# Attention with column norms and a soft mixture of experts on one core: loads of turned v replaced by turns on TensorE, and a new order of all steps

## The chip, the cores and the metric

One core of a Trainium2 chip runs the whole program. The metric is the device time of one execution in microseconds (us). The program is built once; all four engines that compute, and the DMA queue that SP feeds, get their instructions in an order fixed by the source, and only semaphores hold them back.

## The reference, cut to what matters

```python
# q, k, v: (4, 5056, 256); norms and softmax over columns
qn = q / (norm(q, axis=1) + 1e-6);  kn = k / (norm(k, axis=1) + 1e-6)
a  = softmax(kn.T @ qn / tau)                    # (4, 256, 256)
x  = (v @ a).reshape(20224, 256)
logits = x @ phi                                 # 32 slots
d  = softmax over all 20224 rows;  slot_in = d.T @ x
slot_out[e] = relu(slot_in[e] @ w1[e]) @ w2[e]   # 8 experts, 4 slots each
out = softmax over the 32 slots (logits) @ slot_out
```

x is never formed: `logits = v @ (a @ phi)`, and `d.T @ x = (d.T @ v) @ a`.

## The kernel before, in words

Each of the four batches is cut into 10 units of 512 rows of q and k together (1 MB each, tile `raw`, five buffers) and into 5 pieces of 1024 rows of v (1 MB each, tile `v`, six buffers, the last three pieces in buffers of `raw`). For a unit u, ACT squares it (`square`, L203) and rounds its first half to fp32r (`cast`, L182), DVE takes the rest of that half (`low`, L188) and adds the squares up (`add`, L209), and TensorE adds the scores of the four row groups j into the bank `S` (`score`, L226): j = 0, 1 from `hl`, j = 2, 3 from `raw` directly. When a batch's ten units are done, the steps `att_...` turn squares and scores into the 256x256 softmax and into `M`, which is `a @ phi`.

The logits of a piece p (`logits`, L378) need v turned, channels on partitions, in two halves m = 0 and m = 1 (tiles `vt0`, `vt1`, three buffers each; `x` for the last pieces). A half comes in one of two ways. If (p, m) is in the set `LT` (L26), `load_vt` (L130) loads it from a copy of v that the host has turned, 512 KB (480 KB for the last piece of a batch). If not, `turn` (L348) and `turned` (L354) are planned twice, once for each 512 rows: four transposes of 128x128 on TensorE into a bank, and one copy of 128x512 by ACT out of it. After the logits come their running maximum, exponentials, `weights` (L462) and `gather` (L477, the sum of v by slot), and after the last piece `last_slots` and `last_back` (L573): the slots' input.

Then the experts: `up` (L636, needs the tiles of w1), `relu`, `flip_h`, `back_h` (L661; x = 0 on DVE, x = 1 on ACT), `down` (L668; half h needs the loads of w2 of that half), `o_copy`, `o_fold`, `o_back`. Beside them DVE and ACT work on the softmax over slots of each batch b (`c_max`, `c_sub`, `c_exp`, `c_sum`, `c_rec`, `c_mul`, `c_flip`, L578 to L611). Last come the outputs, one tile of 1 MB per piece: `out_mul` (L702) on TensorE, four `out_evict` (L722) shared by ACT and DVE, and `store` (L738). The five pieces of batch 0 are stored in halves, the first half as soon as `o_back(0)` is done.

What sets the order: every step is put into a list `plan` with a key that is not used any more, and the list `ORDER` (L31) is a written-out sequence of positions in `plan`; the last loop calls the steps in that sequence. So the order of each engine's queue is that of `ORDER`, and so is the order in which SP issues the loads and stores. A load takes the buffer of its tag that came free first among the steps already listed, and waits for the last reader of what lay in it.

Of the kernel before, what the change touches and what calls it, by code (L numbers as in the profile page):

```python
# [22 lines left out]
NU = B * UB  # L23
NRAW = 5
NS = [0] + [2] * (NU - 1)
LT = {(p, 0) for p in range(15)} | {(p, 1) for p in range(0, 15, 3)} | {(p, 0) for p in range(15, 20)} | {(10, 1), (13, 1), (15, 1)}  # L26
GR = {b: (3, 2) for b in range(B)}

ORDER = [  # L31
# [46 lines left out]
]  # L78


# [1 line left out]
def colnorm_attention_soft_moe(  # L82
# [671 lines left out]
    def at(key, f, *a):  # L754
        plan.append((key, len(plan), f, a))
# [27 lines left out]
    for p in range(15):  # L783
        for h in range(2):
            for m in range(2):
                if (p, m) in LT:
                    continue
# [67 lines left out]
    for p in range(17):  # L855
        k = (4, 6, 8, 10, 12, 15)[p] if p < 6 else 2 * p + 7
        for h in range(2):
# [3 lines left out]
            if h:  # L861
                for m in range(2):
                    if (p, m) in LT:
                        at(k + h + 0.996 + 0.001 * m, load_vt, p, m)
# [9 lines left out]
    for p in (17, 18, 19):  # L874
        at(NU + 0.99, load_v, p)
        for m in range(2):
            if (p, m) in LT:
                at(NU + 0.99, load_vt, p, m)
    for p in (15, 16, 17, 18, 19):
        for h in range(2):  # L880
            for m in range(2):
                if (p, m) in LT:
                    continue
# [176 lines left out]
```

## Time and profile before

| | us |
|---|---|
| three runs | 288.46, 290.16, 293.66 |
| median | 290.16 |
| span of the profiled execution | 288.4 |

The page gives the profiled execution's span alone as its time, from its first to its last instruction. "Busy" is the time in which an engine had at least one instruction under way; PE is TensorE's matmuls, PEld its loads of weights. A line of the profile is a source line of the kernel. "DMA" is the mean busy share of the core's 16 DMA engines (it can read a little above 1).

### The profile page before, as it was taken

The page shows a single profiled execution, that of the slowest core. Times are in us where ns is not written, and L with a number is a line of the kernel's source. Part 1 is how long each engine was busy: PE and PEld are TensorE (multiplying, and loading weights), DVE is VectorE, ACT ScalarE, POOL GpSimd, SP SyncE. Part 2 cuts the span into 40 slices and gives each one's busy share as a digit, 9 for nine tenths or more (in the row PEclk, how much of TensorE's full clock was granted, in tenths as well). Part 3 has the DMA queues.
Part 4 walks back from the last instruction along what each step waited for, and adds up shares of the span by engine and source line. Part 5 has one row for each costly group of instructions (what it writes and reads, how often), then busy time and mean ns, then how long its engine had stood idle before and what let it go on. Part 6 is the DMA issues. An engine that isn't in the chain of part 4 may idle for free. (4 is left out here: it accounts for less than half of the span.)

```text
span 288.4 us, 6095 instructions
## 1 busy us (share of the span) xinstructions
PE 251.8 (87%) x2452; PEld 203.7 (71%) x2452; DVE 236.4 (82%) x389; ACT 185.1 (64%) x264; POOL 9.8 (3%) x10
## 2 busy tenths in 40 slices
PE   6899999999999999999999999999889898884000
PEld 6689998898888879778788686786554777763000
DVE  1299999899999999999999999988768678994100
ACT  2799887889799796687867957175613426863200
POOL 0000000400004000000200000100000000000000
PEclk9799999999999999999999999999999999998555
DMA  6999999999999999999999999999999997999995
GB/s 206 416 411 421 389 403 427 424 414 418 381 419 367 389 424 424 421 421 422 419 406 419 405 416 427 425 427 417 420 415 413 414 369 311 402 428 413 424 422 245
DMA packets 20188, 115.61 MB, mean 401 GB/s; under 512 B 2368, under 2 KB 2368, under 8 KB 9664
## 3 DMA queue, kind: packets, MB, share of 16 engines
q1 hardware_dynamic: 20160, 115.22, 97.7%
q8 instruction: 19, 0.31, 0.4%
q14 instruction: 9, 0.07, 0.1%
HBM read 94.24 MB, written 20.97 MB: 400 GB/s over the span
## 5 line engine op out<-in xcount | busy, mean ns | idle before, releaser
L203 ACT ACTIVATE sq<-raw 128x2048 f32<-128x2048 f32 x40 | 76.3, 1911 | 18.1 <-DVE sq L209 6.4
L209 DVE TENSOR_TENSOR sq<-sq,sq 128x1024 f32<-128x1024 f32 (+1 forms) x63 | 85.2, 1365 | 1.3 <-ACT sq L203 0.6
L226 PE MATMUL S<-raw 128*128 128x256 f32 x328 | 81.7, 389 | 2.7 <-DMA raw<-in_qk_dram 2.7
L226 PE MATMUL S<-hl 128*128 128x256 f32 x468 | 71.2, 298 | 0.1
L226 PEld LDWEIGHTS S<-raw 128*128 128x128 f32 x328 | 60.1, 194 | 13.4 <-DMA raw<-in_qk_dram 3.5
L226 PEld LDWEIGHTS S<-hl 128*128 128x128 f32 x468 | 61.1, 190 | 3.4 <-issue 1.2
L188 DVE TENSOR_TENSOR hl<-raw,hl 128x1024 fp32r<-128x1024 f32 x39 | 46.8, 1213 | 9.7 <-ACT hl L182 9.7
L182 ACT CAST hl<-raw 128x1024 fp32r<-128x1024 f32 x39 | 40.2, 1042 | 2.6 <-PE S L226 1.7
L736 DVE COPY o<-op_None 128x512 f32<-128x512 f32 x30 | 18.7, 674 | 7.9 <-issue 7.2
L734 ACT COPY o<-op_None 128x512 f32<-128x512 f32 x30 | 15.8, 593 | 12.5 <-issue 8.2
L712 PE MATMUL op_None<-so,cT 32*128 32x256 f32 x240 | 18.6, 401 | 1.9 <-ACT o L734 1.4
L485 PE MATMUL G<-v,dn 128*32 128x256 f32 x320 | 20.1, 382 | 0.1
L712 PEld LDWEIGHTS op_None<-so,cT 32*128 32x128 f32 x240 | 14.6, 184 | 5.6 <-ACT o L734 2.7
L378 PE MATMUL L<-vt,M 128*32 128x256 f32 (+1 forms) x272 | 17.7, 380 | 1.0 <-ACT M L332 1.0
L356 ACT COPY vt<-vTp 128x512 f32<-128x512 f32 x18 | 10.4, 583 | 11.1 <-PE vTp L351 11.1
L248 POOL TENSOR_TENSOR rn<-rn,half 128x4 f32<-128x4 f32 x4 | 9.1, 2263 | 176.2 <-DVE rn L243 176.2
L485 PEld LDWEIGHTS G<-v,dn 128*32 128x32 f32 x320 | 10.0, 109 | 6.5 <-issue 0.5
L351 PE MATMUL vTp<-ident,v 128*128 128x128 f32 x96 | 14.1, 276 | 0.0
L378 PEld LDWEIGHTS L<-vt,M 128*32 128x32 f32 x272 | 8.1, 109 | 7.1 <-ACT M L332 1.5
L351 PEld LDWEIGHTS vTp<-ident,v 128*128 128x128 f32 x96 | 11.0, 142 | 2.4 <-issue 1.2
L399 ACT COPY lt<-L 128x256 f32<-128x256 f32 x20 | 7.2, 372 | 7.6 <-DVE mxs L405 3.4
L734 ACT COPY o<-op 128x256 f32<-128x256 f32 x20 | 6.3, 380 | 8.0 <-PE op L712 8.0
(111 smaller groups left out, 252.8 us busy)
## 6 DMA issues: line engine op xcount, KB each, us to landing
raw<-in_qk_dram SPq DMA_DIRECT2D x39, 1024.0 KB, 9.2
v<-in_v_dram SPq DMA_DIRECT2D x20, 1024.0 KB, 10.6
out_dram<-o SPq DMA_DIRECT2D x15, 1024.0 KB, 12.3
vt<-in_vt_dram SPq DMA_DIRECT2D x21, 512.0 KB, 8.9
w<-in_moe_w_dram SPq DMA_DIRECT2D x8, 1024.0 KB, 14.4
w<-in_moe_w_dram SPq DMA_DIRECT2D x16, 512.0 KB, 11.1
out_dram<-o SPq DMA_DIRECT2D x10, 512.0 KB, 4.2
vt<-in_vt_dram SPq DMA_DIRECT2D x4, 480.0 KB, 10.1
```

The costliest lines, as they stand in the source:

```text
L182: act.copy(hl[:, :ns, 0::2, :], raws[u][:, :ns])
L188: dve.tensor_tensor(hl[:, :ns, 1::2, :], raws[u][:, :ns], hl[:, :ns, 0::2, :].bitcast(F32), op=ALU.subtract)
L203: act.activation(sq, raws[u], AF.Square)
L209: dve.tensor_tensor(a[:, lo:hi], a[:, lo:hi], s[:, lo:hi], op=ALU.add)
L226: pe.matmul(sm, w, x, start=first, stop=False, skip_group_check=True)
L351: pe.transpose(tp[:, P * jj : P * jj + P], vs[p][:, 4 * h + jj, P * m : P * m + P], ident)
L356: act.copy(x[:, h * UT : h * UT + UT], tps[p, h, m])
L378: pe.matmul(L[S * g : S * g + S, :n, :], M[:, m, :], x[:, :n, S * g : S * g + S], start=m == 0, stop=m == 1,)
L485: pe.matmul(gp[S * g : S * g + S, :C], dn[:, x, j, :], vt[:, j, :], start=x == 0 and j < G, stop=x == n - 1 and j >= G,)
L712: pe.matmul(ops[b, p, hf, g][:, h, :], cT[b][S * g : S * g + S, 4 * i : 4 * i + 4, :].rearrange("s j t -> s (j t)"), so[S * g : S * g + S] ...
L734: act.copy(dst, src)
L736: dve.tensor_copy(dst, src)
```

## The change

`LT` gets a term, and `ORDER` is another sequence:

```diff
-LT = {(p, 0) for p in range(15)} | {(p, 1) for p in range(0, 15, 3)} | {(p, 0) for p in range(15, 20)} | {(10, 1), (13, 1), (15, 1)}
+LT = {(p, 0) for p in range(15)} | {(p, 1) for p in range(0, 15, 3)} | {(p, 0) for p in range(15, 20)} | {(10, 1), (13, 1), (15, 1)} - {(3, 1), (6, 1), (9, 1), (10, 1), (13, 1), (15, 1)}
 ORDER = [
-    1, 0, 2, 5, 3, 4, 13, 7, 8, 9, 10, 23, 6, 14, 16, 15, 31, 606, 18, 22, 17, 19, 25, 24, 21, 27, 36, 32, 41, 12,
...
-    991, 1013, 1012, 1009, 1019, 1015, 1020, 1018, 1021,
+    0, 3, 5, 1, 4, 2, 13, 14, 7, 8, 12, 11, 22, 23, 9, 10, 31, 32, 16, 17, 20, 40, 41, 18, 21, 19, 25, 26, 30, 29, 27,
...
+    962, 1025, 1029, 1027, 1026, 983, 985, 987, 986, 1028, 984, 1007, 1009, 1008, 1011, 1010, 964, 1012, 953, 955,
+    957, 954, 988, 956, 958, 1030, 994, 940,
 ]
```

The old list has 1022 positions and the new one 1031. Read back through `plan`, the two give these sequences at the places that the prediction speaks of (qk5 is the load of unit 5, v4 that of piece 4, vt0,1 that of the half (0, 1)):

```
SP's queue, first loads after units 0 to 4
before  qk5 qk6 vt0,1 qk7 vt3,1 qk8 qk9 few qk10 qk11 qk12 v0 qk13 v1 qk14 qk15 qk16 v2 qk17 vt0,0 qk18 vt1,0 vt2,0 qk19 qk20 v3 ...
after   qk5 qk6 qk8 qk7 qk12 few qk9 v4 qk10 v1 qk11 qk15 qk13 qk14 v2 vt0,1 qk16 qk17 qk20 v0 vt0,0 vt1,0 qk18 qk19 vt2,0 vt3,0 qk23 qk21 ...

turns that only the new list has, with the PE steps beside them
 score31,0 turn11,0,1 att_turn2,0 att_turn2,1 turn10,1,1 score33,0 score32,0 turn10,0,1 att_phi2
 score39,3 shift2,0 turn13,1,1 score39,1 score39,0 finish_fold1 score38,2 score35,1 turn13,0,1 finish_slots1
 att_turn3,0 att_turn3,1 turn15,0,1 turn18,1,1 att_phi3 turn15,1,1 logits17

PE from last_slots on
before  up0,0 up0,1 up1,0 flip_h0,1 flip_h0,0 up1,1 down0,0 x3 flip_h1,0 flip_h1,1 down0,0 down1,0 x4 o_fold0
        out_mul0,0 down0,1 out_mul0,1 out_mul0,2 down0,1 out_mul0,3 down0,1 x2 down1,1 x4 out_mul0,4 o_fold1
after   up1,0 up0,1 up0,0 up1,1 flip_h0,1 flip_h0,0 flip_h1,1 flip_h1,0 down0,0 x4 down1,0 x4 o_fold0
        out_mul0,0 out_mul0,1 out_mul0,2 out_mul0,3 down0,1 x4 down1,1 x4 out_mul0,4 o_fold1

DVE from last_back to o_copy0
before  c_flip0,2 c_flip1,0 c_max3 c_sum2 c_sub3 c_flip1,3 c_rec2 back_h0,0 c_flip1,4 c_mul2 back_h1,0 c_flip1,1 c_flip1,2 c_sum3 o_copy0
after   c_flip0,1 c_sub2 c_max3 c_rec1 c_mul1 c_flip1,2 c_flip1,1 c_flip1,3 c_sum2 c_flip1,4 c_flip1,0 back_h0,0 c_sub3 back_h1,0 c_rec2 o_copy0

stores (batch, piece, half)
before  0,0,0 0,1,0 0,2,0 0,3,0 0,4,0 0,0,1 0,1,1 0,3,1 0,2,1 1,0 1,2 1,4 2,1 1,1 1,3 2,3 2,0 0,4,1 2,2 3,1 3,0 2,4 3,2 3,3 3,4
after   0,2,0 0,0,0 0,1,0 0,3,0 0,4,0 0,2,1 0,1,1 2,4 0,3,1 1,4 0,0,1 2,1 3,3 1,0 2,0 3,0 3,2 1,1 1,3 3,1 2,2 1,2 3,4 2,3 0,4,1
```

No function and no buffer count is changed.

## Rows read from the trace of the kernel before

**Rows 1.** The page's parts on busy time and on slices: busy time of each engine with its share of the span and its instructions; the busy share of the DMA engines in 40 slices of 7.2 us.

```profile
PE 251.8 (87%) x2452; PEld 203.7 (71%) x2452; DVE 236.4 (82%) x389; ACT 185.1 (64%) x264; POOL 9.8 (3%) x10
DMA  6999999999999999999999999999999997999995
```

**Rows 2.** Busy time by stage: the stretch, its length, busy us and instructions of PE, PEld, DVE, ACT and POOL, the granted TensorE clock, the DMA share, GB/s.

```profile
20.00:196.00 176.00, 174.89 (x1441) 147.30 (x1440) 171.77 (x248) 136.64 (x169) 9.05 (x4) 1.00 1.01 413
196.00:215.00 19.00, 16.54 (x211) 10.46 (x214) 14.07 (x50) 8.48 (x27) 0.00 (x0) 1.00 1.01 416
...
235.00:245.00 10.00, 9.04 (x198) 7.59 (x194) 7.26 (x21) 4.69 (x15) 0.00 (x0) 1.00 0.82 326
...
255.00:265.00 10.00, 7.45 (x94) 5.88 (x94) 8.01 (x15) 5.15 (x10) 0.00 (x0) 0.97 1.02 424
```

**Rows 3.** All waits of PE and of DVE from 20 to 196 us: who waited for whom, us in total, times, the longest.

```profile
PE L L378 <- ACT M L332: 0.6, 2, 0.4
PE nn L238 <- DVE sq L232: 0.2, 1, 0.2
...
DVE dn L466 <- ACT lt L456: 1.1, 1, 1.1
DVE rn L252 <- POOL rn L248: 0.9, 1, 0.9
```

**Rows 4.** Waits of SP's queue over the whole span, the two largest of the loads of `raw` (L120), in the same columns.

```profile
SPq L120 <- PE S L226: 56.9, 23, 8.7
...
SPq L120 <- DVE hl L188: 31.3, 17, 5.3
```

**Rows 5.** DMA issues by target and size: how many, KB each, median us from issue to landing; and the bytes read and written in all.

```profile
raw<-in_qk_dram SPq DMA_DIRECT2D x39, 1024.0 KB, 9.2
...
vt<-in_vt_dram SPq DMA_DIRECT2D x21, 512.0 KB, 8.9
w<-in_moe_w_dram SPq DMA_DIRECT2D x16, 512.0 KB, 11.1
...
raw<-in_qk_dram SPq DMA_DIRECT2D x2, 256.0 KB, 2.8
```

```profile
HBM read 94.24 MB, written 20.97 MB: 400 GB/s over the span
```

**Rows 6.** PE's instructions in order of time around one turn: start, us from the first start to the last end, instructions merged into one row. A row may start before the one above has ended.

```profile
95.93 0.60 PE L351 MATMUL vTp<-ident,v 128*128 128x128 f32 x4
96.36 1.03 PE L226 MATMUL S<-raw 128*128 128x256 f32 x4
97.04 1.06 PE L226 MATMUL S<-hl 128*128 128x256 f32 x6
```

**Rows 7.** The turns over the whole span, by line: instructions, busy us and mean ns of one, idle time of the engine just before them.

```profile
L351 PE MATMUL vTp<-ident,v 128*128 128x128 f32 x96 | 14.1, 276 | 0.0
...
L356 ACT COPY vt<-vTp 128x512 f32<-128x512 f32 x18 | 10.4, 583 | 11.1 <-PE vTp L351 11.1
```

**Rows 8.** DVE's work on the softmax over slots, and its evictions of the half stores of batch 0, by line, in the same columns.

```profile
L608 DVE STREAM_TRANSPOSE cT<-nat 128x256 f32<-128x256 f32 x20 | 8.6, 431 | 0.0
...
L736 DVE COPY o<-op 128x256 f32<-128x256 f32 x20 | 7.3, 414 | 2.8 <-PE op L712 2.7
...
L598 DVE TENSOR_TENSOR nat<-nat,cs 128x1280 f32<-128x1280 f32 x4 | 5.9, 1474 | 0.0
L583 DVE TENSOR_TENSOR nat<-nat,cm 128x1280 f32<-128x1280 f32 x4 | 5.9, 1473 | 0.0
L590 DVE TENSOR_REDUCE cs<-nat 128x40 f32<-128x1280 f32 x4 | 5.9, 1466 | 0.0
L580 DVE TENSOR_REDUCE cm<-nat 128x40 f32<-128x1280 f32 x4 | 5.9, 1463 | 0.0
...
L595 DVE RECIPROCAL cs<-cs 128x40 f32<-128x40 f32 x4 | 1.6, 403 | 0.1
```

**Rows 9.** All engines in order of time from the last pieces to the second half of the experts' output (a bracket: idle time before, and what ended it).

```profile
196.95 1.07 PE L378 MATMUL L<-vt,M 128*32 128x256 f32 x16 [0.43 <-ACT M L332]
...
214.51 0.19 DVE L574 COPY slT<-slp 128x32 f32<-128x32 f32 x1
...
214.87 5.36 PE L642 MATMUL H<-w,slT 128*32 128x512 f32 x48
...
221.25 1.92 PE L642 MATMUL H<-w,slT 128*32 128x512 f32 x16
...
221.35 0.69 DVE L664 COPY hT<-hTp 128x512 f32<-128x512 f32 x1 [0.81 <-DMA w<-in_moe_w_dram]
...
225.50 2.39 PE L673 MATMUL O<-w,hT 128*32 128x128 f32 x80
...
227.96 0.29 DVE L686 COPY ob<-O 128x128 f32<-128x128 f32 x1
...
229.15 0.73 PE L712 MATMUL op<-so,cT 32*128 32x128 f32 x16 [0.35 <-ACT so L694]
...
235.26 1.67 PEld L673 LDWEIGHTS O<-w,hT 128*32 128x32 f32 x60 [0.37 <-DMA w<-in_moe_w_dram]
```

**Rows 10.** SP's queue in order of time: the last loads and the first stores.

```profile
201.87 23.64 SPq L631 DMA_DIRECT2D w<-in_moe_w_dram  x15
230.76 12.80 SPq L744 DMA_DIRECT2D out_dram<-o  x9
```

86 rows, old and new, of the table ORDER are left out of this document.

## Prediction

> **What bounds the kernel now.** I read the page's slices first. The DMA engines are at nine tenths or more in nearly every slice [rows 1], and by stage their share is 1.01 at 413 to 424 GB/s wherever loads or stores stand ready [rows 2]. So bytes set a floor. Next the engines: from 20 to 196 us PE has a matmul under way for 174.89 of 176.00 us and DVE is busy for 171.77 [rows 2], and the list of waits gives PE 0.8 us in all and DVE 2.0 [rows 3]. So in this stage DMA, PE and DVE are all full at once; ACT, at 136.64, is not.
>
> Which of them has cover? A 1 MB load of `raw` lands 9.2 us after its issue [rows 5], while 1.05 MB at 0.42 MB/us takes 2.5: 6.7 us are the queue ahead of it. SP waits for buffers nearly always (56.9 us for PE's last score of a unit, 31.3 for DVE) [rows 4]. The loads run as far ahead as five buffers let them, and PE hardly ever waits for one.
>
> At the end the order matters. The last part of w2 ends PE's last wait at 235.26 [rows 9]; from there 20.97 MB of stores at 424 GB/s take 49.5 us [rows 2, 5], and 235 to 245 us runs at a share of 0.82, so 1.8 us are lost there. 235.2 + 49.5 + 1.8 = 286.5, and 1.9 remain to the span of 288.4: the end. The median of the three runs is 290.16, 1.8 above the span, and I add that to each sum.
>
> **The change, part by part.** First, how many loads go. Python's `-` binds before `|`, so the subtracted set acts on the last term alone and empties it: (3,1), (6,1), (9,1) come back in through the second term. **Three** loads are dropped. The lengths of the list agree: a half that is turned has four steps in place of one, and 1031 − 1022 = 9 is three halves.
>
> *DMA:* three times 512 KB, 1.57 MB; at 0.42 MB/us −3.7 us. The w2 loads would land at 231.5 if nothing else held the stream.
>
> *PE:* six turns more, 24 transposes. One turn starts at 95.93 and the next instruction at 96.36: 0.43 us [rows 6], so 6 × 0.43 = 2.6. The two of piece 15 lie beside `att_phi3`, before logits that waited 0.43 us for ACT's M [rows 3, 9], and are costed at nothing; if M is ready by then they cost 0.9. The four others fall where PE never waits: **+1.7 us** by the time of `last_back`. The row of transposes has a mean of 276 ns each [rows 7], but four in a row take 0.43 to the next issue, as they overlap. The Trainium skill, "TensorE: Matmul & The Clock Gate", section "Part 4: PE-mode transpose", gives about 275 ns for one 128x128 transpose in a kernel; by that, added up, 24 would take 6.6 us and not 2.6. As a duration the trace agrees with it (276), and the starts here decide.
>
> *ACT:* six copies of 583 ns [rows 7], 3.5 us, hidden in the 39 us for which ACT stands idle in that stage [rows 2]. A bank's next turn may wait for one; the copy's wait for PE is ACT's idle time (11.1 us) and not PE's.
>
> *DVE:* no work added. c_sub2, c_rec1 and c_mul1 (1.47 + 0.40 + 1.47 = 3.3 us [rows 8]) move from before `last_back` to behind it, so ahead of it DVE has 3.3 us less, PE sets the pace alone, and DVE will wait for it.
>
> *Loads in a new order:* SP's queue stands behind every buffer that is not free. Units 12, 15, 20 and 23 are asked for earlier than they are used, each holding one of five buffers. 176 us hold some 38 units, 4.6 us each; one buffer held for one unit makes later loads 4.6 us late, and the cover is 6.7. So one hold costs nothing, two together up to 2.5 us. I take nothing; the upper end is a rival below. POOL's four operations, which DVE awaited for 0.9 us [rows 3], keep their place.
>
> *The experts:* `last_back` was at 214.51 [rows 9], now 216.2. From there to `back_h`(0,0) DVE had three flips, three big operations and a reciprocal: 3 × 0.43 + 3 × 1.47 + 0.40 = 6.1 us, which is the 221.35 of before with its wait of 0.81. It now has six flips, four big ones and a reciprocal, 8.9 us [rows 8]: 225.1. The ups (5.36 + 1.92 us of PE [rows 9]) and two flips are done by 224.7, so DVE decides, if narrowly; ACT's c_exp2, now ahead of all `relu`, waits only for the second of those DVE steps. Then back_h0,0 (0.69), c_sub3 and back_h1,0 end at 228.0, and `down` of the second half of the hidden units runs behind them (64 matmuls at 2.39/80 us, 1.9 us). `o_copy`(0) goes from 227.96 to about 230.3, the first `out_mul` from 229.15 to 231.5.
>
> *Stores in a new order:* the queue's first was piece 0's half, at 230.76 [rows 10]. Now it is piece 2's, and the ready pieces 0 and 1 stand behind it. Three pieces need six evictions by DVE: 231.5 + 0.73 for the first `out_mul` [rows 9] + 6 × 0.414 [rows 8] = 234.7 at the earliest; with a breath between for PE and ACT up to 237. I take 236.
>
> *Sum:* loads are through by 231.5 or somewhat later, and DMA idles until 236. Then 2.1 us until bytes flow (256 KB landed in 2.8 us [rows 5], 0.7 of it transfer), 49.5 of stores, 1.9 of end: 289.5, which is 1.1 above the span of before, and with the 1.8 to the median **291.0 us**. The saving of 3.7 us in bytes is real, and it is turned into idle time ahead of the first store. A stall of up to 4.5 us in the load stream costs nothing, for the same reason.
>
> **Rivals.** *PE has headroom, and the bytes come through.* For it: "busy" counts pipelined matmuls, and the engine's weight loads are under way for 147.30 of 176 us only [rows 2]. Then `last_back` stays where it was, a first store near 232 follows, and 288.4 − 3.7 = 284.7, with 1.8 makes 286.4. Over 2% (below 284.4; 2% is what a measurement of this kernel can tell) it comes only if the 1.8 us lost from 235 to 245 go as well. Against it: waits of 0.8 us [rows 3], and DVE's 2.8 us more behind `last_back`. The Trainium skill, "Perfetto Trace Analysis", section "Identifying the Most-Contended Engine", says that matmul busy time is a bad measure of how near a kernel is to its limit and that the share of weight loads is a better one. By it PE would have 28 us free there and this rival would be the forecast; that PE is never seen waiting speaks against it here.
>
> *The output stage starves further.* DVE has c_mul2, c_sum3, c_mul3 and a dozen flips between its first evictions, and stores of one piece wait for those of others: 3 to 5 us, a span of 292 to 294, 294 to 296 at the median.
>
> *Slower: SP's queue is blocked by early units.* The place is the change of batch (units 12 ahead of 9, 15 ahead of 13, 20 ahead of 18, 23 ahead of 21). If holds overlap, three of them at 2.5 us each make PE wait 7.5 us for `raw`, on the path: 297.0, and **298.5 to 299 us**. It decides from the point where PE's waits for `raw` from 20 to 196 us pass 6 us. For it: SP already waits for buffers nearly always [rows 4], so nothing takes up a lost one. Against: PE's waits now are 0.8 us, and the new order of PE's steps has moved with the loads (unit 12's load comes early, and so may its use).
>
> *Six loads dropped*, as the minus sign seems to say: −7.4 us of DMA, +5.2 of PE. The list's length excludes it; no chance.
>
> **How the numbers follow.** Forecast 0.45 (289 to 293); headroom 0.18, of which 0.06 falls below 284.4; starved output 0.16, of which 0.03 passes 296.0; blocked SP 0.21, of which 0.20 does. So faster 0.06, same 0.71, slower 0.23. The range is 286 to 298: it takes in the forecast with first stores from 234.7 to 237 and the turns at 1.7 to 2.6, most of the headroom case and of the starved one, and the lower part of the blocked one.
>
> **What would show it.** The page should list 18 loads of 512 KB of `vt` (21 before), 120 transposes in place of 96, and 24 copies in place of 18. From 20 to 196 us PE's waits stay under 3 us and DVE's rise above 3. The last w2 load lands before 234 us, PE no longer waits for it, and the DMA share between 230 and 238 falls below 0.6. The first store is issued at 235 to 237. PE waiting for `raw` by more than 6 us would prove the blocked queue; DMA shares of 0.8 or less from 240 to 260 the starved output; a first store before 233 the headroom. I am wrong most simply if the new order saves or costs PE time in the main stage that its waits don't show.

## The result and the profile after

The changed kernel takes **291.11 us** in the median of 20 runs (289.15 to 293.23), the kernel before 289.93 in as many (288.35 to 293.66). The ratio is 1.0052, 95% interval 1.003 to 1.0074: no change by the bound of 2%, and half a per cent slower beyond its interval. The medians lie 1.2 us apart and the two profiled executions, with spans of 288.2 and 288.4 us, hardly at all: what the two traces show is not a difference in length but two ways to the same length. The traces of runs 1, 5, 8 and 11 below are of executions that were slow for their kernel (290.87, 297.31, 290.09 and 294.83 us), so lengths are compared by medians and ratios, and rows of these four serve for the order of events.

The page of the changed kernel, its parts on busy time, on slices and on issues:

```profile
PE 255.9 (89%) x2476; PEld 209.0 (73%) x2476; DVE 238.2 (83%) x389; ACT 187.9 (65%) x270; POOL 11.3 (4%) x10
...
DMA  7999999999999999999999996999999989999997
...
HBM read 92.67 MB, written 20.97 MB: 394 GB/s over the span
...
vt<-in_vt_dram SPq DMA_DIRECT2D x18, 512.0 KB, 9.4
```

Against [rows 1, 5]: three loads of 512 KB fewer (18 for 21), 1.57 MB less read, and one slice of DMA that reads 6 where it stood at 9. By stage, in the columns of [rows 2]:

```profile
20.00:196.00 176.00, 173.84 (x1456) 148.68 (x1459) 170.30 (x244) 140.82 (x179) 10.65 (x4) 1.00 0.99 399
172.00:176.00 4.00, 4.00 (x31) 3.82 (x30) 3.74 (x9) 3.22 (x7) 0.00 (x0) 1.00 1.01 413
176.00:180.00 4.00, 4.00 (x56) 2.84 (x58) 4.00 (x4) 3.40 (x3) 0.00 (x0) 1.00 0.43 132
196.00:215.00 19.00, 18.60 (x218) 10.90 (x219) 16.38 (x54) 8.08 (x25) 0.00 (x0) 0.92 1.01 423
...
232.00:236.00 4.00, 3.80 (x108) 3.49 (x112) 3.66 (x7) 2.63 (x7) 0.00 (x0) 1.00 0.78 304
...
235.00:245.00 10.00, 8.70 (x199) 7.27 (x190) 8.51 (x21) 3.69 (x12) 0.00 (x0) 1.00 0.97 383
```

Two things stand out. From 176 to 180 us DMA moves at 0.43 of its time, so 4 × 0.57 = 2.3 us are lost, where the kernel before had a share of 1.00:

```profile
176.00:180.00 4.00, 4.00 (x54) 2.61 (x51) 4.00 (x5) 2.54 (x6) 0.00 (x0) 1.00 1.00 420
```

And from 196 to 215 PE is busy for 18.60 us of 19, where it was 16.54 [rows 2]. The hole is explained by SP's queue from 164 to 185 us, its waits, and then its issues:

```profile
SPq L133 <- DVE sq L208: 6.8, 1, 6.8
SPq L127 <- PE S L225: 4.0, 1, 4.0
```

```profile
166.37 4.74 SPq L127 DMA_DIRECT2D v<-in_v_dram  x2
177.93 0.33 SPq L133 DMA_DIRECT2D x<-in_vt_dram  x1
178.31 0.90 SPq L127 DMA_DIRECT2D v<-in_v_dram  x2
...
203.83 21.84 SPq L630 DMA_DIRECT2D w<-in_moe_w_dram  x15
233.55 8.47 SPq L743 DMA_DIRECT2D out_dram<-o  x7
```

The load at 177.93 is the half (18,0). It goes into a buffer of squares (`x`) and stands 6.8 us in the queue until DVE has read them, while pieces 16 and 17 wait behind it. The queue ahead of DMA runs dry. The last w2 load is issued at 225.3 and lands 10.0 us later, at **235.36**: where it landed before (235.22), although 3.7 us of bytes were taken out ahead of it.

The output stage, all engines in order of time:

```profile
211.49 0.19 DVE L573 COPY slT<-slp 128x32 f32<-128x32 f32 x1
211.85 9.87 PE L641 MATMUL H<-w,slT 128*32 128x512 f32 x64
216.38 0.16 PEld L641 LDWEIGHTS H<-w,slT 128*32 128x32 f32 x8 [1.10 <-DMA w<-in_moe_w_dram]
222.85 0.69 DVE L663 COPY hT<-hTp 128x512 f32<-128x512 f32 x1 [2.82 <-PE hTp L657]
226.63 1.95 PE L672 MATMUL O<-w,hT 128*32 128x128 f32 x62 [0.24 <-DMA w<-in_moe_w_dram]
228.64 0.29 DVE L685 COPY ob<-O 128x128 f32<-128x128 f32 x1 [2.57 <-PE O L672]
```

`last_back` comes at 211.49, three us earlier than before [rows 9]. Then the weight loads of the ups wait for w1 (1.10 us) and the downs for w2 (0.24), DVE idles, and `o_copy`(0) is at 228.64, 0.7 later than before. By these rows it is the load stream that sets the pace behind `last_back`, and the last w2 load that lets the stores through; the runs below test it.

### The profile page after: what moved, and what is told of

Same layout as the page of the kernel before. It is cut to its first block, busy times and chain, and to the rows that moved or that the text cites. A ratio compares the mean times of both kernels' runs of the same rounds, so it can differ in the third digit from the quotient of the medians.

```text
span 288.2 us, 6117 instructions
## 1 busy us (share of the span) xinstructions
PE 255.9 (89%) x2476; PEld 209.0 (73%) x2476; DVE 238.2 (83%) x389; ACT 187.9 (65%) x270; POOL 11.3 (4%) x10
## 3 DMA queue, kind: packets, MB, share of 16 engines
HBM read 92.67 MB, written 20.97 MB: 394 GB/s over the span
## 4 chain that ended last, share of the span: by engine, by line
PE 32%; DMA 27%; DVE 20%; ACT 6%; issue 6%; POOL 3%; SPq 0%; DVEq 0%; ACTq 0%
PE S L225 12%; DMA w<-in_moe_w_dram 10%; DMA raw<-in_qk_dram 10%; DVE sq L208 9%; PE op_None L711 5%; DVE hl L187 5%; DMA x<-in_vt_dram 4%; PE G L484 3%; PE L L377 3%; DVE o L735 3%; DMA vt<-in_vt_dram 3%; POOL rn L247 3%; ACT sq L202 2%; PE op L711 2%; PE O L672 2%
## 5 line engine op out<-in xcount | busy, mean ns | idle before, releaser
L225 PE MATMUL S<-raw 128*128 128x256 f32 x328 | 80.7, 386 | 2.7 <-DMA raw<-in_qk_dram 2.6
L225 PEld LDWEIGHTS S<-raw 128*128 128x128 f32 x328 | 59.2, 192 | 11.9 <-DMA raw<-in_qk_dram 4.1
L187 DVE TENSOR_TENSOR hl<-raw,hl 128x1024 fp32r<-128x1024 f32 x39 | 47.2, 1217 | 10.2 <-ACT hl L181 10.2
L711 PE MATMUL op_None<-so,cT 32*128 32x256 f32 x240 | 20.6, 426 | 7.4 <-ACT o L733 4.4
L711 PEld LDWEIGHTS op_None<-so,cT 32*128 32x128 f32 x240 | 16.0, 202 | 11.1 <-ACT o L733 9.8
L350 PE MATMUL vTp<-ident,v 128*128 128x128 f32 x120 | 17.5, 274 | 0.5 <-ACT vt L355 0.5
L355 ACT COPY vt<-vTp 128x512 f32<-128x512 f32 x24 | 13.9, 584 | 6.2 <-PE vTp L350 6.1
L247 POOL TENSOR_TENSOR rn<-rn,half 128x4 f32<-128x4 f32 x4 | 10.6, 2662 | 174.5 <-DVE rn L242 83.2
L350 PEld LDWEIGHTS vTp<-ident,v 128*128 128x128 f32 x120 | 14.3, 144 | 2.1 <-ACT vt L355 0.9
L711 PE MATMUL op<-so,cT 32*128 32x128 f32 x160 | 9.2, 292 | 1.8 <-ACT so L693 0.8
## 6 DMA issues: line engine op xcount, KB each, us to landing
w<-in_moe_w_dram SPq DMA_DIRECT2D x16, 512.0 KB, 10.2
```

The lines of the kernel that those rows point to most:

```text
L187: dve.tensor_tensor(hl[:, :ns, 1::2, :], raws[u][:, :ns], hl[:, :ns, 0::2, :].bitcast(F32), op=ALU.subtract)
L225: pe.matmul(sm, w, x, start=first, stop=False, skip_group_check=True)
L247: pool.tensor_tensor(rn, rn, half, op=ALU.pow)
L350: pe.transpose(tp[:, P * jj : P * jj + P], vs[p][:, 4 * h + jj, P * m : P * m + P], ident)
L711: pe.matmul(ops[b, p, hf, g][:, h, :], cT[b][S * g : S * g + S, 4 * i : 4 * i + 4, :].rearrange("s j t -> s (j t)"), so[S * g : S * g + S] ...
```

## The experiments

Two theories stood against each other. The **output theory** is the prediction's: the saved bytes turn into idle DMA ahead of a late first store. The **queue theory**: the saved bytes were lost earlier, in SP's queue, and the load stream sets the end. All edits are of the order of steps, and in runs 4, 5, 11 and 12 also of which halves are loaded and which turned; what moves is shown in the queue in which it moves. Each ratio is to the kernel before, run beside that run.

**1. The load of (18,0) behind pieces 16 and 17.**

```diff
 SP: v18
-vt18,0
 v16 v17
+vt18,0
 w2_1,0
```

> The changed kernel with one step moved: SP issues the load of the half (18,0) behind those of pieces 16 and 17, not ahead of them. In the changed kernel it held SP's queue until 177.9 us, and the DMA share fell to 0.43 from 176 to 180 (2.3 us lost). Queue theory (the bytes saved were lost in the load stream, and the landing of the last w2 load at 235.4 sets the end): the hole closes, the last w2 load lands near 233, the time falls by 2.3 us to about 288.8. Output theory (as in the prediction: the first store sets the end): the hole closes, the first store is still issued at 233.5, the DMA share from 232 to 236 falls from 0.78 to about 0.3, the time stays at 291.1.

Measured: 289.26 us, ratio to before 0.9973 (0.9944 to 1.0003) where the change has 1.0052: 0.8%, 2.3 us. Stages and SP's queue of this run:

```profile
176.00:180.00 4.00, 4.00 (x62) 2.73 (x64) 3.97 (x5) 2.89 (x3) 0.00 (x0) 1.00 1.01 428
...
228.00:232.00 4.00, 3.48 (x71) 2.78 (x68) 3.09 (x7) 2.92 (x7) 0.00 (x0) 0.95 0.61 243
...
268.00:276.00 8.00, 2.84 (x40) 1.65 (x36) 4.27 (x7) 3.62 (x7) 0.00 (x0) 0.93 0.69 286
```

```profile
203.31 19.44 SPq L632 DMA_DIRECT2D w<-in_moe_w_dram  x15
231.24 4.24 SPq L745 DMA_DIRECT2D out_dram<-o  x4
```

The hole is gone, the last w2 load lands at 232.45, and with it the first store moves, from 233.55 to 231.24. The output theory had it stay at 233.5. It does not, as the ups ahead of it had been waiting for these very loads (run 7 shows how much that is). Now DMA runs short of stores instead, with a share of 0.61 from 228 to 232 us. (The 0.69 from 268 to 276 is taken up in run 8.)

**2. Stores in the order of their evictions, first try.**

```diff
 SP: w2_5,1
+store0,0,0 store0,1,0
 w2_7,1
-store0,2,0 store0,0,0 store0,1,0
+store0,2,0
```

> The changed kernel with SP's first three stores in the order of their evictions: pieces 0, 1, 2 and not 2, 0, 1. Both theories: the first store is issued near 231.4 in place of 233.5. Output theory: the end comes 2 us earlier, about 289.0. Queue theory: the stores' bytes wait behind the last w2 load until 235.4, so only what is lost from 232 to 236 (0.9 us at a share of 0.78) can come back: 290.2 to 291.1.

Measured: 294.41 us, 1.0166 (1.0133 to 1.02). The first store is issued at 230.7, but my move put two stores ahead of the last w2 load, which then waited in SP's queue for the evictions: issued at 232.15 instead of 225.3, landed at 238.4, and the second half of the downs came 2.8 us later (end of the last at 240.37 for 237.55). It says nothing on the theories, and much on the price of one load behind waiting stores: 3.3 us.

**3. Both.** The edits of 1 and 2 together, with the same flaw.

> Both moves together. If the two stand in series (each alone hidden behind the other), this gives what neither gives alone: last w2 load near 233, first store near 231.4, DMA share from 232 to 236 above 0.9, time 288.5 to 289.0. If the queue alone decides: the same as the first of these runs. If the output alone decides: the same as the second.

Measured: 294.34 us, 1.0171 (1.0141 to 1.02). Nothing follows but that the flaw outweighs the gain of 1.

**4. The old order with the loads changed.** The three loads go out of the kernel before; each of the six turns is put where its piece has landed and ACT has room, such as:

```diff
 PE: att_cols3
+turn15,0,1
 score38,3 score39,1
+turn15,1,1
 score37,0
```

> The kernel before in its own order, with the three loads dropped and the six turns put in: the change of the loads without the new order. By the prediction's steps: DMA has 3.7 us less, last_back comes 1.7 us later (216.2), the last w2 load lands by 232, the first store is issued at 232.5 and its bytes flow from 234.6, so 0 to 0.6 us are gained on the 289.9 of before. If PE has headroom: last_back stays at 214.5, the first store at 230.8, and 3.7 us come through: 286.2. If SP's queue gives the bytes back: the last w2 load still lands near 235, and the time is 290 to 291.5.

Measured: 290.25 us, 1.0048 (1.0026 to 1.0069). Here the prediction's sequence is to be seen:

```profile
176.00:180.00 4.00, 4.00 (x54) 2.49 (x46) 4.00 (x5) 2.97 (x6) 0.00 (x0) 1.00 0.77 277
...
232.00:236.00 4.00, 3.77 (x96) 2.87 (x89) 3.49 (x10) 1.66 (x5) 0.00 (x0) 1.00 0.39 152
```

```profile
217.04 0.19 DVE L575 COPY slT<-slp 128x32 f32<-128x32 f32 x1
...
233.31 11.93 SPq L745 DMA_DIRECT2D out_dram<-o  x9
```

`last_back` is 2.5 us later than [rows 9] (forecast 1.7, upper end 2.6), the first store at 233.31 (forecast 232.5), the last w2 load lands at 233.3 (forecast by 232), and DMA idles at 0.39 ahead of the stores: 2.4 us of the bytes given back there. But not all of the 2.5 us is the price of the turns. The logits of piece 19, in the kernel before and in this run, and then the granted clock of this run:

```profile
203.19 1.06 PE L378 MATMUL L<-x,M 128*32 128x256 f32 x16 [0.64 <-PE gt L506]
```

```profile
204.35 1.06 PE L379 MATMUL L<-x,M 128*32 128x256 f32 x16 [0.64 <-PE gt L507]
```

```profile
206.00:208.00 2.00, 1.78 (x5) 0.94 (x6) 1.70 (x9) 1.68 (x7) 0.00 (x0) 0.59 0.98 406
208.00:210.00 2.00, 2.00 (x16) 0.97 (x18) 1.53 (x6) 1.00 (x4) 0.00 (x0) 0.56 1.01 416
```

All six turns lie ahead of these logits, and they are 1.2 us late. The other 1.3 us come where the granted clock is 0.59 and 0.56, in a stretch in which it was 1.00 before; no turn stands there. About one more was lost from 176 to 180 (0.77), where SP stood 7.5 us for a buffer of `vt0`.

**5. The new order with the loads kept.** The three loads right behind the other half of their pieces, no turns of these.

```diff
-turn10,0,1 turn10,1,1 turn13,0,1 turn13,1,1 turn15,0,1 turn15,1,1
 SP: vt10,0
+vt10,1
```

> The changed kernel's order with the three loads kept (each right behind the other half of its piece) and without the six turns: the new order alone. If the load stream sets the end (queue theory), 3.7 us more bytes come on top of the hole at 176 to 180 us: last w2 load near 238 to 239, time 293 to 294.5. If PE sets it, six turns fewer give 1.7 to 2.6 us back: 288.5 to 289.5.

Measured: 292.9 us, 1.0106 (1.007 to 1.0142), just below what the queue theory expects and more than 3 us beyond the other. So the new order alone costs about 1%, and dropping the loads wins about half a per cent back in it (the two intervals just touch), while in the old order (run 4) it costs half a per cent.

**6. Stores in the order of their evictions, behind the last w2 load.**

```diff
 SP: w2_7,1
+store0,0,0 store0,1,0
-store0,2,0 store0,0,0 store0,1,0
+store0,2,0
```

> The changed kernel with the first three stores in the order of their evictions (pieces 0, 1, 2), this time all behind the issue of the last w2 load. Output theory: the first store is issued near 231.5, the time falls by 2 us to 289. Queue theory: the last w2 load stays at 235.4 and the stores' bytes wait for it, at most 0.9 us come back: 290.2 to 291.1.

Measured: 292.21 us, 1.0091 (1.0059 to 1.0123). No gain; the intervals of this and of the change overlap. The first store was issued at 231.92, 1.6 us earlier than in the change, and its bytes waited for w2, which landed at 235.84. With the hole in place, the first store is not what the end waits for.

**7. The late load and the stores together, without the flaw.** The edits of 1 and 6.

> The late load of (18,0) and the three stores in eviction order, behind the last w2 load. With the late load alone the last w2 load landed at 232.5, the first store was issued at 231.2, and the DMA share from 228 to 232 was 0.61. If the first store is what DMA then waits for, it is issued near 229.2 and 1 to 1.5 us more are gained: about 288. If the evictions and stores behind it decide, nothing changes: 289.3.

Measured: 289.66 us, 1.0013 (0.9977 to 1.0049), no different from run 1 (0.9973, 0.9944 to 1.0003). The first store was issued at 229.09, 2.1 us earlier than in run 1, and it brought nothing that can be measured: with the hole closed it is not what the end waits for either. Against run 6, which differs from this one by the late load alone, run 7 is run 1 over again: 1.0091 becomes 1.0013, 0.8% with intervals that don't touch. The stretch from 176 to 180 us in run 6, then in run 7:

```profile
176.00:180.00 4.00, 4.00 (x50) 3.21 (x53) 4.00 (x7) 3.82 (x4) 0.00 (x0) 1.00 0.29 86
```

```profile
176.00:180.00 4.00, 4.00 (x66) 2.63 (x68) 3.96 (x4) 2.40 (x3) 0.00 (x0) 1.00 1.01 425
```

The last w2 load lands at 233.0 for 235.8, and the first store comes 2.8 us earlier: 1.4 up to `last_back` (210.50 for 211.91), and 1.4 from there to `back_h`(0,0) (220.64 for 223.45), where PE's wait for w1 in the ups is 0.54 us for 1.44; behind that the two run alike. So the output theory fails for the change, and the price of the early load is measured twice.

**8. The late load, and the old order behind `last_back`.** Everything from the ups to the last store stands as in the kernel before, and so do, on SP, the loads of w1 and w2 but for two; the three steps c_rec(1), c_mul(1) and c_sub(2) come first on DVE.

```diff
 SP: edit of 1
-PE: up1,0 up0,1 up0,0 up1,1 flip_h0,1 flip_h0,0 flip_h1,1 flip_h1,0 down0,0 x4
+PE: up0,0 up0,1 up1,0 flip_h0,1 flip_h0,0 up1,1 down0,0 x3 flip_h1,0 flip_h1,1 down0,0
-store: 0,2,0 0,0,0 0,1,0
+store: 0,0,0 0,1,0 0,2,0
```

> The changed kernel with the late load of (18,0) up to last_back, and everything behind last_back in the order that the kernel before had (ups, downs, softmax over slots, evictions, stores, and the last w1 and w2 loads). If, once the hole is filled, the new order of the output stage is what loses (1.6 us from 228 to 232, 1.8 from 236 to 240, 2.5 from 268 to 276 in the run with the late load alone), the losses after 260 go and the time falls to 286 to 287.5. If the output stage is not the limit, it stays at 289.3 or above.

Measured: **287.35 us**, 0.9926 (0.9897 to 0.9955), faster than both kernels, and 0.5% faster than run 1, whose interval it just touches. Since the w loads moved too, this is the price of the whole new order behind `last_back` and not of the evictions alone. The end of the output stage, in the changed kernel, run 6 and run 7 (new order), and then in run 10 below (old order):

```profile
268.00:276.00 8.00, 2.01 (x32) 1.54 (x32) 3.23 (x6) 2.93 (x6) 0.00 (x0) 0.84 0.94 393
```

```profile
268.00:276.00 8.00, 3.49 (x56) 2.69 (x48) 5.13 (x9) 4.20 (x8) 0.00 (x0) 0.93 0.76 315
```

```profile
268.00:276.00 8.00, 0.63 (x12) 0.22 (x6) 2.31 (x4) 1.84 (x4) 0.00 (x0) 0.72 0.93 388
```

```profile
268.00:276.00 8.00, 0.00 (x0) 0.00 (x0) 1.29 (x2) 1.56 (x3) 0.00 (x0) 0.50 1.02 426
```

In the old order DMA is full there: PE has nothing left, and five evictions remain. In the new order PE still has 12 to 56 matmuls of the outputs to do, and 0.5 to 1.9 us of DMA are lost. The 2.5 us that the expectation took from run 1 are above all three. Where the rest of the 0.5% lies was not traced.

**9. The three DVE steps back ahead of `last_back`, in the changed kernel.**

```diff
 DVE: c_sum1
+c_rec1 c_mul1
 att_sum3
 ...
+c_sub2
 maxima of piece 15
 last_back c_flip0,1
-c_sub2
 c_max3
-c_rec1 c_mul1
```

> The changed kernel with c_rec(1), c_mul(1) and c_sub(2) put back ahead of last_back (behind the sums of piece 14 and ahead of the logits of piece 15), as the kernel before had them: 3.4 us of DVE leave the stretch from last_back to the first back_h and go ahead of it. If DVE set the pace ahead of last_back before the change, last_back comes up to 3.3 us later (211.5 to 214.8), and the time goes up by as much as the w2 loads don't cover it, 291 to 293. If that DVE work was in nobody's way there, last_back stays at 211.5; back_h(0,0) waits for PE's ups and the w1 loads as it does now (222.9), so the time stays at 291.

Measured: 294.0 us, 1.0163 (1.012 to 1.0206), 1.1% above the change. PE's waits from 196 to 215 us, which are 0.2 in the changed kernel, and `last_back`:

```profile
PE rp L421 <- DVE mx L416: 2.2, 1, 2.2
PE L L379 <- ACT M L333: 0.9, 1, 0.9
```

```profile
215.31 0.19 DVE L575 COPY slT<-slp 128x32 f32<-128x32 f32 x1
...
225.57 0.69 DVE L665 COPY hT<-hTp 128x512 f32<-128x512 f32 x1 [5.30 <-PE hTp L659]
```

PE stands behind the maximum of piece 15 to 17, and that behind c_sub(2) on DVE: 211.49 becomes 215.31. Behind `last_back` DVE then idles for 5.30 us. Not all of the 3.8 us is DVE's. PE's step behind that maximum starts at 201.75 for 199.43, 2.3 us late; the other 1.5 us come from 202 to 206 us, where in this execution the granted clock fell (it is 1.00 in the changed kernel's there):

```profile
202.00:204.00 2.00, 2.00 (x16) 1.85 (x19) 1.45 (x8) 1.40 (x3) 0.00 (x0) 0.64 1.03 434
204.00:206.00 2.00, 2.00 (x24) 1.01 (x20) 0.99 (x4) 1.72 (x8) 0.00 (x0) 0.51 1.01 426
```

So the move of these 3.4 us is worth 2.3 us at `last_back` in these two traces, and 1.1% of the time by the medians.

**10. The same in the kernel of run 8.** The edit of 9 on it.

> The same three DVE steps put back in the kernel that has the late load of (18,0) and the old order behind last_back. There back_h(0,0) came 9.2 us after last_back, behind DVE. If last_back stays where it is, back_h(0,0) and the first store come 1 to 2 us earlier and the time falls below the 287.4 of that kernel, to about 286.5. If last_back moves by the 3.4 us instead, the two cancel: 287.4 to 288.5.

Measured: 291.68 us, 1.0074 (1.0042 to 1.0106): 1.5% above run 8, more than either expectation. `last_back` moved from 212.00 to 214.13, and the first store from 229.89 to 232.07 with it; PE's wait for the maximum is 2.2 us as in run 9, and the granted clock stays at 1.00 up to `last_back`. The two traced executions are of nearly equal length (290.09 and 290.18 us), so they don't show how 2.1 us become 1.5%, which is 4.3.

**11. The old order with the loads changed, and (16,0) loaded later.**

```diff
 SP: v17
-vt16,0
 v18 v16 vt18,0
+vt16,0
```

> The old order with the three loads dropped and six turns put in, and the load of (16,0) behind those of pieces 18 and 16 and of (18,0). In the old order SP stood 7.5 us for a buffer of vt0 there and DMA lost 1.4 us between 176 and 186. Queue theory: the loss goes and the w1 and w2 loads land about 1.4 us earlier (w2 at 232 in place of 233.3). As the first store was issued at 233.3 there, behind a last_back at 217.0, no more than 0.5 us of it can reach the end: 289.7 to 290.3. If the loads alone set the end, 288.9.

Measured: 291.81 us, 1.0065 (1.0035 to 1.0094), not to be told from run 4. The loss did not go (share 0.80 from 170 to 185 us, 0.91 in run 4): with (16,0) out of the way piece 18, and then 16, waited for buffers too. This one load's place does not mend it; whether another's would was not tried. Inconclusive on the rest.

**12. The kernel of run 8 with the three loads kept.** The edit of 5 on it.

> The kernel with the late load of (18,0) and the old order behind last_back (287.4 us, 0.9926 of before), with the three loads kept and without the six turns: what the dropped loads are worth once the load stream has no hole and the output stage keeps up. If the saved bytes come through there, keeping the loads costs 2 to 3.7 us: 289.4 to 291. If they are given back in any order, because PE's turns cost as much or because buffers hold the stream, the time stays at 287 to 288.

Measured: 290.11 us, 1.0026 (0.9998 to 1.0055), against 0.9926: there the dropped loads are worth 1.0%, 2.9 us, most of the 3.7 us of their bytes. The traces also tell what the six turns cost in the new order. `last_back` in run 12, which has none of them, in runs 7 and 8, which have all six, and in run 10, which has all six and the three DVE steps ahead of `last_back` as in the kernel before:

```profile
210.69 0.19 DVE L574 COPY slT<-slp 128x32 f32<-128x32 f32 x1
```

```profile
210.50 0.19 DVE L575 COPY slT<-slp 128x32 f32<-128x32 f32 x1
```

```profile
212.00 0.19 DVE L575 COPY slT<-slp 128x32 f32<-128x32 f32 x1
```

```profile
214.13 0.19 DVE L575 COPY slT<-slp 128x32 f32<-128x32 f32 x1
```

Against run 7 that is nothing, against run 8, whose trace is one of the four named with the result, 1.3 us. And with the turns but without the move on DVE the new order has `last_back` no later than the kernel before (214.51).

## Why the prediction was right, and where it was not

The time (291.0 against 291.11), the direction and the three loads in place of six came out as forecast. **But three steps failed, one of them to the one side and two to the other, and by luck they cancelled.** The sum itself has a slip: 236 + 2.1 + 49.5 + 1.9 = 289.5, and with the 1.8 that is 291.3, not 291.0.

**Three loads, six turns.** Right: 18 loads of 512 KB, 92.67 MB for 94.24, 120 transposes, 24 copies. ACT's part is hidden as forecast (140.82 of 176 us, and one wait of PE for a copy, 0.5 us). From 20 to 196 us PE's waits are 1.9 us (forecast under 3) and DVE's 3.6 (above 3).

**The bytes: "the w2 loads would land at 231.5 if nothing else held the stream".** Something did. 2.3 of the 3.7 us went into the hole at 176 to 180 us (runs 1 and 7 give them back). The other 1.4 are not traced; there are stretches with a full share and a lower rate, 369 and 350 GB/s between 22 and 36 us, and 407 for 418 from 100 to 170, which may hold them. The failed step is the sentence that a stall of up to 4.5 us in the load stream costs nothing: it took w2's last landing for the only one that matters, while the ups and downs need each w1 and w2 load as it lands. A stall at 178 moves all of them.

**PE: +1.7 us by `last_back`.** This step failed to the other side. In the old order six turns cost 1.2 us by the logits of piece 19 (run 4; the rest of its 2.5 us goes with the clock). In the new order they cost nothing to 1.3 (runs 7, 8 and 12), and `last_back` with them is no later than before even without the move on DVE (214.13 in run 10 for 214.51), so the new order makes up for them. It is what the prediction named as the simplest way to be wrong, PE time in the main stage that its waits don't show. Where the new order finds it stays open; one place may be the first 20 us, in which PE is busy for 17.2 to 17.9 us in the traces of the change and of runs 7, 10 and 12, and for 16.24 and 15.36 in those of the kernel before and of run 4 (but for 16.63 in that of run 9, which has the new order).

**DVE: "PE sets the pace alone".** So did this one. I counted the 3.4 us that left the stretch ahead of `last_back` as nothing and charged them behind it. Runs 9 and 10 show that in the new order they stand in the way there: PE's wait for the maximum grows from 0.2 to 2.2 us in both, which moves `last_back` by 2.1 to 2.3 us, and the time by 1.1% and 1.5%. [Rows 2] gave the hint: from 196 to 215 us PE is busy for 16.54 of 19, and the waits of the kernel before in that stretch include DVE:

```profile
PE gt L506 <- DVE gs L500: 0.7, 1, 0.7
PE rp L420 <- DVE negm L440: 0.5, 1, 0.5
```

I read PE's waits from 20 to 196 only [rows 3] and carried them on.

**The output stage.** `last_back` forecast 216.2, measured 211.49; `back_h`(0,0) 225.1 and 222.85, and it waits for PE's flips (2.82 us), not for DVE's longer queue; `o_copy`(0) 230.3 and 228.64; the first store 236 and 233.55, earlier than the range of 234.7 to 237. The DMA share from 230 to 238 was to fall below 0.6 and was 0.90, with 0.78 from 232 to 236. The last w2 load was to land before 234 and landed at 235.36.

**The sum** put the end at a first store of 236 with w2 long landed. Measured is a last w2 load at 235.36 with the stores nearly ready. Both leave about 53 us to the end, hence the agreement. My mechanism is in part that of the loads' change in the old order (run 4: the late first store, with 2.4 us of idle DMA ahead of it), and not that of the whole change.

**The rivals.** *Headroom of PE*: half right. In the old order the turns delay the last logits by 1.2 us and the bytes don't come through. In the new order they delay `last_back` by 1.3 us at most, and with the hole closed and the old order behind `last_back` 2.9 of the 3.7 us do come through (run 12 against 8), as this rival has it; in the change, with the hole and the new order of the output stage, dropping the loads is worth 0.5% (run 5). That `last_back` is early is DVE's part. The weight loads' share, 148.68 of 176 us for 147.30, does not tell the two orders apart. *Blocked SP*: half right. PE's waits for `raw` were 1.4 us from 20 to 196, far below the 6 that were to prove it. But a load asked for too early did block the queue, at another place, and took the gain instead of adding a loss. *Starved output*: not in the changed kernel (0.97 from 235 to 245 us), but it is next in line: with the hole closed DMA is at 0.68 from 232 to 236 and at 0.85 from 236 to 240 us (run 7), and the old order behind `last_back` is worth another 0.5% (run 8 against run 1, whose intervals just touch).

The runs also form a path from the kernel before to the change, on which each step changes one part and the parts add up:

| step | ratio after it | worth |
|---|---|---|
| three loads for six turns, old order (run 4) | 1.0048 | +0.5% |
| new order ahead of `last_back`, without the early load of (18,0) and the move on DVE (run 10) | 1.0074 | +0.3%, intervals overlap |
| the three DVE steps behind `last_back` (run 8) | 0.9926 | −1.5% |
| new order behind `last_back`, w loads with it (run 1) | 0.9973 | +0.5%, intervals just touch |
| (18,0) loaded early (the change) | 1.0052 | +0.8% |

So the half per cent is the balance of one clear gain, the move on DVE, and of losses that together outweigh it; the new order of the 196 us ahead of the last pieces costs nothing that is clear of noise. What a part is worth depends on where on the path it is taken: the dropped loads cost 0.5% at the start of it and gain 1.0% at run 8 (run 12). Whether it is the move on DVE or the new order that lets the loads come through, no run tells.

## What to carry to other kernels

Bytes taken out of a saturated load stream are a gain only if the queue that issues the loads can use the time: look for the load that waits longest for its buffer, and at what stands behind it. Where an engine shows no waits in the long stage, read its idle time again in the short serial stage that follows, since work that was free in the one may sit on the path in the other. A total that comes out as forecast proves no step of it; the times of the landmarks on the way (here `last_back`, the last w2 load, the first store) do. And where several parts change at once, undo them along one path from the old kernel to the new: the parts then add up, and a part that helps only in company is seen.

## What was not expected of the hardware

In the changed kernel's profile the granted clock fell behind `last_back`, when the ups began, as the windows show:

```profile
210.00:212.00 2.00, 1.85 (x18) 1.73 (x22) 1.49 (x9) 0.04 (x1) 0.00 (x0) 1.00 1.05 442
212.00:214.00 2.00, 2.00 (x12) 0.44 (x10) 2.00 (x3) 0.70 (x2) 0.00 (x0) 0.52 0.95 395
214.00:216.00 2.00, 2.00 (x12) 0.38 (x4) 1.93 (x4) 1.33 (x2) 0.00 (x0) 0.63 1.03 412
216.00:218.00 2.00, 1.94 (x18) 0.55 (x20) 1.97 (x5) 0.07 (x1) 0.00 (x0) 1.00 1.00 408
```

At 0.52, near the lower level of 1.2 GHz, PE did 12 of the ups' matmuls in 2 us where it does 24 at the full one (218 to 220 us of the same trace), although it had been busy for 1.85 of the 2 us ahead. It cost next to nothing here: in run 6 the clock was full in that stretch, PE stood 1.44 us for w1 in the ups instead, and they ended 10.2 us after the end of `last_back` as against 10.0.

It is not always so cheap. The two falls shown with runs 4 and 9 came ahead of `last_back`, on the path, and cost 1.3 and 1.5 us in their traces. Nor does the same sequence of steps always bring one: in run 9 PE was busy for 0.25 us from 200 to 202, waiting for the maximum, and then the clock fell to 0.64 and 0.51; in run 10 it was busy for 0.00 us in the same 2 us, and the clock stayed at 1.00 up to 214. A landmark that moves in one trace should be read beside the granted clock of the stretch ahead of it, or the clock's part is put down to the edit.
